# One mask product per score bank, two projection tiles behind the attention, and MLP buffers and weights placed earlier, in a transformer block on one core

## The chip, the cores and the metric

The kernel runs on one core of a Trainium2 chip. The metric is the time of one execution on the device in microseconds (us); the median over several executions counts. The engines are TensorE (PE, matrix products; its weight loads are PEld), VectorE (DVE), ScalarE (ACT), GpSimd (POOL) and SyncE (SP), whose work here is to issue transfers. Each engine takes its instructions in the order in which they were written for it, and waits at an instruction until what it needs is there; what stands behind it on the same engine waits too.

## The reference

One token sequence, S = 2048 rows of D = 576 floats, goes through an attention layer and a mixing layer with an MLP. The layer norms are modulated by six vectors that come from a condition:

```
sa, ca, ga, sb, cb, gb = split(silu(c) @ w_mod)
h = layernorm(x) * (1 + ca) + sa
q, k, v = split(h @ wqkv)                       # 32 heads of 18
p = softmax(q k^T / sqrt(18)), only 0 <= i - j < 256
x = x + ga * ((p v) @ wo)
h = layernorm(x) * (1 + cb) + sb
g = gelu(layernorm(h) @ w1)                     # 4 channel groups shifted by +1, -1, +2, -2 rows
x1 = h + shifted(g) @ w2
x = x + gb * (x1 + gelu(layernorm(x1) @ w3) @ w4)   # w3: 576 x 4608, w4: 4608 x 576
```

All is float32, and most products use operands split into a high and a low part, three products in place of one.

## The kernel before

**Stages.** By the trace they lie, in us from the start of the span: the q, k, v projections about 10 to 228; attention 228 to 738; mixing with the output projection's last tiles 740 to 958; the MLP for the first 1024 rows 958 to 1426; the MLP for the second 1024 rows 1426 to 1885. Intermediate rows go through tensors in HBM (qd, kd, vd, od, xp, hbd, xnd, xmd, rd).

**Order by a table of times.** The program has no scheduler. Every step is a small function that is entered with `at(time, function)`; at the end all entries are sorted by their time and called, and each appends its instructions to its engines' queues. The times only set an order. Inside attention the unit is one step of the head loop: `tm(h)` is the time of step h, HU = 13 units long. In the mixing stage a pair of 128-row tiles has 17.7 units, and in the MLP a block of columns has U = 24.2.

**Attention.** A step n (there are 32) is a group of 512 queries (g = n // 8) and four heads, taken as two halves j. For each half TensorE computes products mx (L448, with a mask Mq added by a product with the identity, L450), VectorE takes their maxima (L460), TensorE transposes these (mt, L468), and SyncE stores them into two rows of the query tile (L477), so that the scores proper come out with the maximum subtracted. About two steps later the scores X are computed in five PSUM banks (`xm`): each bank holds one to three key blocks (BANKS), a product each (L492), and then the mask is added: products of the identity `identr` with pieces of the mask tile Mk, which holds two 64-column halves, written over the ends of the key blocks (L517). ScalarE exponentiates each bank (L522). With all five banks there are nine mask products in a half, 576 in all. The score banks are s0 and s1 in turn. The products with the values (av, L544) follow two steps later, in banks s2 and s3, then the transposes of the outputs (ot, L554), and SyncE stores od (L566).

The query tiles have four buffers and the key tiles three. `load(n)` (L423, L425) brings both to SBUF, and POOL makes masked copies from them, QS (L431) and KS (L438), on which the mx and X products wait.

**Output projection.** `wotile(t, h)` enters all steps of one 128-row tile t: its rows from od (`orow`, L599 to L602), five transposes pa and pb (L608, L610), their evacuation into a high and a low part T (L615, L617), two halves of 14 products wo (L629), the residual (L633), two layer norms, and three stores (L655, L658, L661). Tiles 0 to 11 are entered with attention at h = 12.4 + 2t, tiles 12 to 15 with the mixing stage. All use banks s2 and s3.

**Mixing.** W1 and W2 are loaded (w1r, L740; w2r) and split into high and low parts (L752 to L757). For each pair of tiles the normalised rows come back (xmr, L780), are transposed (ptm, L787), multiplied with W1 (pg, L808), put through gelu and shifted (Gm), and multiplied with W2 (w, L857). VectorE adds the result to h (x, L861); ScalarE normalises it (xm, L873); POOL multiplies it with the gate and adds the residual (L877, L878); SyncE stores xmd (L881) and rd (L884).

**MLP.** The hidden layer is cut into 18 blocks, each of two 128-column pieces; for each block, seven products of combined rows A and combined weights W3 (u0P and so on, L1090) are added up in different ways (L1096) to the four results, a Strassen-like scheme. Gelu (L1111) and a split (L1113, L1120) give G; down products d (L1143) with W4 are added to eight accumulators acc (L1151). The raw weights of a block go through one buffer, wf (L970, L971; W4 at L975): POOL makes four differences (L982), ScalarE the high parts (L988 for W3, L1017 for W4), POOL the low parts (L994, L1023) and the gate on W4 (L1008), and VectorE a low tail (L1002). `wprep(jj, ...)` enters the preparation of block jj and the W4 part of the block before. Blocks are numbered through both halves: 0 to 17, and 18 to 35 backwards over the columns, so that block 18 reuses the W3 and W4 of block 17 and block 19 is the first that needs new W3 weights. Between the halves, `pair(1, i, ...)` loads the next 1024 token rows (rows, L1043) into the same wf buffer, POOL combines them (L1051 to L1061), and TensorE transposes them into A (pt, L1071, L1072).

## Time and profile before

| | us |
|---|---|
| median of 3 executions | 1880.74 (1880.45 to 1882.55) |
| profiled execution | 1886.33 |
| its span | 1884.5 |
| TensorE busy | 1755.3, 13752 products |
| VectorE, POOL, ScalarE busy | 1090.4, 897.1, 709.1 |
| mean granted TensorE clock | 0.963 of full |

The profile is of one execution. A busy share over the whole span mixes stages; what counts is how long TensorE stands at each place, who releases it, and at which clock it works. In the rows of a timeline the columns are: start, duration, engine, line, operation, output and inputs, shape, number of instructions in the row, and in brackets the idle time ahead of it with what ended it. The start of one product to the start of the next is what it costs in a stream; the duration of a row is longer, because products are pipelined.

### The profile page before, as it was taken

What the parts mean: (1) busy time and instruction counts of PE and PEld (TensorE: products, weight loads), DVE (VectorE), ACT (ScalarE), POOL (GpSimd) and SP (SyncE); (2) the same over time, 40 slices, a digit from 0 to 9 for tenths busy, and PEclk for the clock granted to TensorE, in tenths of its full rate; (3) what the DMA queues carried; (4) which work ended last, traced back from release to release, by engine and by line L of the source; (5) the groups of instructions that cost most, each with busy time, mean ns of one, the idle gap of its engine ahead of it and who ended that gap; (6) DMA issues with size and microseconds to landing.
All of it is one profiled execution on the core that took longest, in us unless ns stands there. A gap on an engine that the chain in (4) does not pass through costs nothing.

```text
span 1884.5 us, 34263 instructions
## 1 busy us (share of the span) xinstructions
PE 1755.3 (93%) x13752; PEld 1610.3 (85%) x13752; DVE 1090.4 (58%) x1800; ACT 709.1 (38%) x1210; POOL 897.1 (48%) x843
## 2 busy tenths in 40 slices
...
GB/s 144 316 174 182 163 145 90 117 111 131 157 131 142 146 111 103 198 204 167 122 161 58 56 58 55 57 58 57 57 69 141 59 59 59 60 59 60 58 44 51
DMA packets 156134, 206.75 MB, mean 110 GB/s; under 512 B 19012, under 2 KB 87620, under 8 KB 155400
## 3 DMA queue, kind: packets, MB, share of 16 engines
...
q14 instruction: 50, 0.41, 0.1%
...
## 4 chain that ended last, share of the span: by engine, by line
PE 45%; DVE 4%; ACT 2%; POOL 2%; issue 1%; DMA 1%; SPq 1%; DVEq 0%; POOLq 0%
PE d L1143 23%; DVE W L1002 1%; PE w L857 1%; PE pg L808 1%; PE u20P L1090 1%; PE u32P L1090 1%; PE u31P L1090 1%; PE u30P L1090 1%; PE u29P L1090 1%; PE u24P L1090 1%; PE u23P L1090 1%; PE u22P L1090 1%; PE u21P L1090 1%; PE u15P L1090 1%; PE u14P L1090 1%
## 5 line engine op out<-in xcount | busy, mean ns | idle before, releaser
L1143 PE MATMUL d<-W,G 128*128 128x288 f32 x3456 | 509.3, 298 | 13.4 <-DVE acc L1151 10.5
L1143 PEld LDWEIGHTS d<-W,G 128*128 128x128 f32 x3456 | 490.4, 190 | 35.4 <-DVE acc L1151 10.9
L1151 DVE TENSOR_TENSOR acc<-d,acc 128x576 f32<-128x576 f32 x288 | 216.7, 753 | 196.7 <-PE d L1143 194.0
L982 POOL TENSOR_TENSOR wf<-wf 128x384 f32<-128x384 f32 x140 | 144.1, 1051 | 337.0 <-DMA wf<-in_B_w_dram 328.2
L460 DVE TENSOR_REDUCE m<-mx 128x2 f32<-128x640 f32 x224 | 181.0, 817 | 171.4 <-PE mx L450 169.8
L522 ACT ACTIVATE P<-X 128x512 f32<-128x512 f32 (+4 forms) x320 | 181.9, 572 | 227.4 <-PE X L517 226.2
L448 PE MATMUL mx<-KD,QS 128*128 128x320 f32 (+4 forms) x512 | 168.0, 378 | 28.0 <-POOL QS L431 18.4
L492 PE MATMUL X<-QD,KS 128*128 128x64 f32 (+2 forms) x704 | 155.8, 312 | 1.2 <-ACT P L522 0.7
L431 POOL TENSOR_SCALAR QS<-QD,rowm 128x512 fp32r<-128x512 f32 x128 | 87.6, 697 | 145.2 <-DMA QD<-qd 51.9
L994 POOL TENSOR_TENSOR W<-wf,W 128x768 fp32r<-128x768 f32 x70 | 150.0, 2167 | 1.2 <-ACT W L988 1.2
L1120 DVE TENSOR_TENSOR G<-U,G 128x512 fp32r<-128x512 f32 x108 | 91.2, 845 | 98.8 <-ACT G L1113 98.8
L1111 ACT ACTIVATE U<-U 128x512 f32<-128x512 f32 x108 | 68.4, 633 | 184.1 <-DVE U L1096 184.1
L448 PEld LDWEIGHTS mx<-KD,QS 128*128 128x128 f32 x512 | 103.7, 202 | 34.4 <-POOL QS L431 19.5
L1111 ACT ACTIVATE C<-C 128x512 f32<-128x512 f32 x36 | 22.7, 632 | 287.3 <-DVE C L1096 287.3
L278 PE MATMUL qk<-hT,Wqk 128*128 128x512 f32 x504 | 121.3, 402 | 0.0
L278 PEld LDWEIGHTS qk<-hT,Wqk 128*128 128x128 f32 x504 | 96.1, 192 | 24.3 <-issue 0.9
L517 PE MATMUL X<-Mk,identr 128*128 128x128 f32 (+1 forms) x576 | 112.3, 269 | 0.0
L492 PEld LDWEIGHTS X<-QD,KS 128*128 128x128 f32 x704 | 108.9, 199 | 2.5 <-ACT P L522 1.8
L1008 POOL TENSOR_TENSOR wf<-wf,gb 128x1152 f32<-128x1152 f32 x35 | 104.0, 2971 | 13.3 <-DVE acc L1151 6.8
L438 POOL TENSOR_SCALAR KS<-KD,rowm 128x768 fp32r<-128x768 f32 (+1 forms) x128 | 107.6, 853 | 0.0
L1023 POOL TENSOR_TENSOR W<-wf,W 128x1152 fp32r<-128x1152 f32 x35 | 95.6, 2731 | 13.8 <-ACT W L1017 13.8
L450 PE MATMUL mx<-Mq,identr 128*128 128x128 f32 x448 | 102.0, 228 | 0.0
...
## 6 DMA issues: line engine op xcount, KB each, us to landing
...
```

Source lines behind the costliest of these rows:

```text
L278: nc.tensor.matmul(po, W[:, a, fs], H[:, c, :], start=(n == 0), stop=(n == 13))
L438: nc.gpsimd.tensor_scalar(t[:, b0:, r], src[:, b0:], M[:, 2 + r:3 + r], 0.0, op0=ALU.mult, op1=ALU.add)
L448: nc.tensor.matmul(pm[:, s, 320 - 64 * nb:320], lhs, K[:, j, 64 * (i + 5 - nb):64 * (i + 5)], start=True, stop=False)
L460: nc.vector.tensor_reduce(out=m[:, c:c + 2], in_=pm[:, :, 0:320], axis=mybir.AxisListType.X, op=ALU.max, negate=True)
L492: nc.tensor.matmul(px[:, c:c + q1 - q0], K[:, b + 4].rearrange("p r k -> p (r k)"), Q[:, j, q0:q1], start=(i == 0), stop=False)
L517: nc.tensor.matmul(o, self.identr, mv, start=False, stop=(i == len(ops) - 1))
L522: nc.scalar.activation(p[:, lo:], X["px", n, j, k][:, lo:], AF.Exp, scale=SCALE)
L982: nc.gpsimd.tensor_tensor(out=WF[:, o], in0=WF[:, a], in1=WF[:, b], op=ALU.subtract)
L994: eng.tensor_tensor(out=W[:, s0:s1, 3:5, :], in0=WF[:, 1 + s0:1 + s1, 0:2], in1=W[:, s0:s1, 0:2, :].bitcast(F32), op=ALU.subtract)
L1090: nc.tensor.matmul(po, W[:, w - 1, a, :], X[:, b, :], start=(m == 0), stop=(m == 6))
L1143: nc.tensor.matmul(po, G[:, g, ta, b, ts], W[:, w, b, cs], start=(n == 0), stop=(n == 5))
L1151: nc.vector.tensor_tensor(out=a, in0=po, in1=a, op=ALU.add)
```

## The change

1. **Masks.** Mk grows from two to five 64-column pieces (k0, k1, 0, k0, k1; one copy on VectorE more). `xm` adds the mask of a whole bank with one product: a new function `cut` returns for each bank the output columns and the piece of Mk. In four banks these are two runs of 128 columns (in the second bank of the first eight steps two of 64), in the fifth a single run. 576 products become 320. In some banks the piece k1, 0 or 0, k0 is used so that a run is 128 wide where only 64 need a mask. An unused zero tile and function are removed.
2. **End of attention.** Tiles 10 and 11 are entered at h = 33.95 and 34.5 (before 32.4 and 34.4) with banks s0 and s1, tile 12 at 35.22, tiles 13 to 15 at T1 + 6.7, 18.2 and 35.9. The mixing stage begins at tm(34.07) (before tm(34.95)), its first tile pair T1 is 19 units behind that. W1 loads come at once, the splits 5.5 units later than before, the W2 steps 5 later; the gate row gb is loaded at 15.
3. **MLP start.** The MLP begins 4 units after the last mixing pair (before 11). VectorE's tail of block 0's weights is moved behind tile 13's evacuations. The row, residual and normalised tiles of tile 15 lie in the space of the accumulators 1 to 3, in the pool m2 that is open earlier, and U1 to U3 in m2 too. The pool m3 opens, and the mixing pool closes, a little after the MLP's first step. Five accumulators are loaded at 0.2 U and three at 0.4 U.
4. **Between the halves.** `wprep` of block 19, together with the W4 part of block 17, is entered 0.3 U before block 17 (before: at 1.9 U after, with W4 alone at -0.35 U). The row loads, combinations and transposes of the second half have new times.

```diff
-        self.Mk = c.tile([P, 2, 64], F32R, name="Mk")
+        self.Mk = c.tile([P, 5, 64], F32R, name="Mk")
...
+        nc.vector.tensor_copy(self.Mk[h, 3:5], self.Mk[h, 0:2].bitcast(F32))
...
-            for i, (o, mv) in enumerate(ops):
-                nc.tensor.matmul(o, self.identr, mv, start=False, stop=(i == len(ops) - 1))
+            o, mv = cut(px, g, k, self.Mk)
+            nc.tensor.matmul(o, self.identr, mv, start=False, stop=True)
+
+        def cut(t, g, k, M):
+            pairs = lambda c, st: AP(t[:, 0:1].tensor, t[:, c:c + 1].offset, [t[:, 0:1].ap[0], (st, 2), (1, 128)])
+            mk = lambda a, w: M[:, a:a + w].rearrange("p a b -> p (a b)")
+            split = lambda m: m.rearrange("p (a b) -> p a b", a=2)
+            both = mk(0, 2).unsqueeze(1).to_broadcast([P, 2, 128])
+            sz = split(mk(1, 4))
+            if g:
+                return ((pairs(0, 256), sz), (pairs(128, 256), split(mk(0, 4))), (pairs(0, 320), both), (pairs(64, 320), both), (t[:, 192:320], mk(0, 2)))[k]
+            return ((pairs(0, 256), sz), (pairs(192, 256)[:, :, 0:64], M[:, 1:4:2]), (pairs(64, 256), sz), (pairs(128, 256), sz), (t[:, 256:320], mk(1, 1)))[k]
...
-        def otT(t):
+        def otT(t, b0):
...
-        for t in range(12):
+        for t in range(10):
             wotile(t, 12.4 + 2 * t)
-        return tm(34.0 + LX - 1.1), wotile
+        return tm, wotile
...
-            at(T0 + .1 + k, w1load, k)
-            at(T0 + 2 + 1.5 * k, w1split, k)
-            at(T0 + 12 + 2 * k, w2load, k)
-            at(T0 + 14 + 2 * k, w2split, k)
+            at(T0 + .1 + .1 * k, w1load, k)
+            at(T0 + 7.5 + 1.5 * k, w1split, k)
+            at(T0 + 17 + 2 * k, w2load, k)
+            at(T0 + 19 + 2 * k, w2split, k)
+        at(T0 + 15, lambda: nc.sync.dma_start(self.gb, self.modd[5].to_broadcast([P, D])))
...
-        return T1 + TB * (NG - 1) + 8.5, e + 11.0
+        return T1 + TB * (NG - 1) + 8.5, e + 4.0
...
+            self.late = lambda n, name: p.tile([P, D], F32, tag=f"acc{n}", name=name, bufs=1)
...
-        for i, f in enumerate((whi(0, 0, 3), wlo(0, self.nc.gpsimd, 0, 3), whi(0, 3, 7), wtail(0, self.nc.vector), wlo(0, self.nc.gpsimd, 3, 7))):
+        for i, f in enumerate((whi(0, 0, 3), wlo(0, self.nc.gpsimd, 0, 3), whi(0, 3, 7), wlo(0, self.nc.gpsimd, 3, 7))):
             at(Tc + .04 + .01 * i, f)
+        at(T0 - 7.7, wtail(0, self.nc.vector))
         add(wprep(1, 1, 0, T0 - 4.0, 11.0))
-        at(T0 - .02, begin3)
+        at(T0 + .35, begin3)
         for k in range(8):
-            at(T0 + .2 * U + .01 * k, ainit(0, (k + 4) % 8))
+            at(T0 + (.2 if k < 5 else .4) * U + .01 * k, ainit(0, (k + 4) % 8))
...
-                at(t - 0.35 * U, wload(jj + 1, None, j))
-                at(t - 0.2 * U, w4gb(jj))
-                at(t + 0.005 * U, w4hi(jj))
-                at(t + 0.01 * U, w4lo(jj))
+                if sb + 1 < SB:
+                    at(t - 0.301 * U, lambda a=jj: Ws.__setitem__(a + 1, Ws[a]))
+                    add(wprep(jj + 2, js[-2], j, t - 0.3 * U, 0.9 * U, jj))
+                else:
+                    at(t - 0.35 * U, wload(jj + 1, None, j))
...
-                    add(wprep(jj + 2, js[-2], None, t + 1.9 * U, 0.55 * U))
+                    for i, (tl, ts, td, tt) in enumerate(((.40, .52, .60, .66), (.41, .62, .92, .98), (.92, 1.06, 1.24, 1.30), (1.25, 1.38, 1.56, 1.62))):
+                        pair(1, i, t + tl * U, t + ts * U, t + tt * U, 0.25 * U, t + td * U)
...
-            T1 = te + 18.0
-            wotile(12, 35.45)
-            for i in range(3):
-                wotile(13 + i, (T1 + 17.7 * i + .5 - t1 - 6.0) / HU - 0.3)
+            T1 = te + 19.0
+            wotile(10, 33.95, 0)
+            wotile(11, 34.5, 0)
+            wotile(12, 35.22)
+            for i, d in enumerate((6.7, 18.2, 35.9)):
+                wotile(13 + i, (T1 + d - tm(0)) / HU - 0.3)
```

The change moves instructions at three places that matter below; line numbers of the changed kernel differ a little from those of the kernel before. First SyncE at the end of attention. Before (od_99 is the last group's output, od_98 in the first `or` rows the third group's; w1r are rows of W1, xmr the first mixing tiles, `or` and xr the rows of a projection tile):

```order
L566 DMA od_99<-o_9504 128x4x144
L731 DMA gb<-modd_151 128x576
L740 DMA w1r_9558<-in_B_w_dram 128x576
L740 DMA w1r_9576<-in_B_w_dram 128x576
L599 DMA or_9578<-od_99 128x576
L600 DMA or_9578<-od_99 128x64
L602 DMA xr_9581<-in_A_x_dram 128x576
L740 DMA w1r_9588<-in_B_w_dram 128x576
L740 DMA w1r_9590<-in_B_w_dram 128x576
```

and of the change (od_98 is now the last group's output, od_97 the third's):

```order
L721 DMA w1r_9188<-in_B_w_dram 128x576
L723 DMA w1r_9190<-in_B_w_dram 64x576
L724 DMA w1r_9190<-in_B_w_dram 64x576
L761 DMA xmr_9262<-xnd_131 128x576
L762 DMA xmr_9262<-xnd_131 128x64
L761 DMA xmr_9265<-xnd_132 128x576
L762 DMA xmr_9265<-xnd_132 128x64
L548 DMA od_98<-o_9234 128x4x144
L581 DMA or_9287<-od_98 128x576
```

The store of the last attention output, and behind it tile 12's rows, stood ahead of most of W1 and of the mixing tiles; they now stand behind all of W1 and the first two mixing tiles.

Second, SyncE at the start of the MLP, behind the loads of tile 15 (x_15, rr). Before:

```order
L843 DMA x_15_11955<-hbd_131 128x576
L865 DMA rr_11972<-xp_115 128x576
L881 DMA xmd_167<-xm_12000 128x576
L884 DMA rd_183<-rr_11877 128x576
L881 DMA xmd_168<-xm_12046 128x576
L970 DMA wf_12064<-in_B_w_dram 128x2x128
```

and of the change:

```order
L824 DMA x_15_11696<-hbd_130 128x576
L846 DMA rr_11713<-xp_114 128x576
L954 DMA wf_11747<-in_B_w_dram 128x2x128
L955 DMA wf_11747<-in_B_w_dram 128x1x128
...
L959 DMA wf_11747<-in_B_w_dram 128x2x576
L862 DMA xmd_166<-xm_11743 128x576
L865 DMA rd_182<-rr_11620 128x576
L862 DMA xmd_167<-xm_11801 128x576
```

The weights of block 1 (wf) stood behind the stores of tiles 13 and 14 (xmd, rd); they now stand ahead of them.

Third, SyncE between the halves of the MLP. Before, the last wf row ahead of the token rows (rows) is block 17's W4 alone, and block 19's weights come behind the output stores:

```order
L975 DMA wf_15438<-in_B_w_dram 128x2x576
L975 DMA wf_15579<-in_B_w_dram 128x2x576
L1043 DMA rows_15684<-xmd_162 128x576
L1044 DMA rows_15684<-xmd_166 128x576
L1043 DMA rows_15684<-xmd_163 128x576
L1044 DMA rows_15684<-xmd_167 128x576
```

and of the change:

```order
L959 DMA wf_15181<-in_B_w_dram 128x2x576
L954 DMA wf_15331<-in_B_w_dram 128x2x128
L955 DMA wf_15331<-in_B_w_dram 128x1x128
...
L959 DMA wf_15331<-in_B_w_dram 128x2x576
L1028 DMA rows_15482<-xmd_161 128x576
L1029 DMA rows_15482<-xmd_165 128x576
```

The eight pieces of block 19's W3 are in the same transfer group as block 17's W4, ahead of the rows that take over the buffer.

83 lines of the change are left out of this document (27 added, 56 removed).

## The prediction

> **What bounds the kernel now.** I read the busy shares first, then the table of stretches, then TensorE's waits, and last the timelines around the places that the change touches.
>
> ```profile
> PE 1755.3 (93%) x13752; PEld 1610.3 (85%) x13752; DVE 1090.4 (58%) x1800; ACT 709.1 (38%) x1210; POOL 897.1 (48%) x843
> ```
>
> No engine but TensorE is near its limit. So time is won by TensorE work that goes, by stretches in which TensorE stands, and by the halved clock that follows such stretches. The stretches say where these are (columns: stretch, then for each engine its busy time and instructions, the granted TensorE clock, the DMA share and GB/s):
>
> ```profile
> 240.00:300.00 60.00, 55.78 (x412) 52.95 (x412) 26.73 (x60) 20.61 (x44) 35.01 (x42) 0.63 0.47 132
> 300.00:400.00 100.00, 86.93 (x1155) 80.14 (x1154) 46.58 (x79) 41.08 (x84) 40.54 (x56) 0.91 0.43 114
> 400.00:500.00 100.00, 95.01 (x1246) 89.60 (x1245) 60.91 (x105) 47.13 (x89) 45.21 (x67) 1.00 0.47 136
> ...
> 740.00:780.00 40.00, 26.55 (x176) 24.51 (x175) 18.79 (x42) 16.68 (x38) 15.20 (x20) 0.83 0.63 183
> ...
> 940.00:980.00 40.00, 24.28 (x127) 21.29 (x126) 18.53 (x33) 10.12 (x12) 29.19 (x26) 0.83 0.52 175
> ...
> 1440.00:1460.00 20.00, 15.34 (x63) 12.62 (x64) 10.80 (x14) 8.56 (x12) 8.91 (x7) 0.66 0.23 70
> 1460.00:1480.00 20.00, 17.38 (x94) 15.61 (x93) 15.46 (x17) 5.46 (x8) 11.17 (x7) 0.91 0.24 70
> ```
>
> Attention runs to about 738 us. Its later part (400 to 500) is full at full clock; its first (240 to 400) has holes and a lower clock. The other holes stand at the three joints: attention to mixing (740), mixing to MLP (940), first to second half of the MLP (1440). TensorE's waits (line, who released it; total us, times, longest) name the same places:
>
> ```profile
> PE mx L448 <- POOL QS L431: 18.4, 7, 3.4
> ...
> PE wo L629 <- DVE T L617: 10.3, 10, 7.0
> ...
> PE u0P L1090 <- ACT U L1103: 9.0, 1, 9.0
> ...
> PE u19P L1090 <- POOL W L994: 3.1, 1, 3.1
> ...
> PE u19P L1090 <- DVE W L1002: 2.6, 1, 2.6
> ```
>
> **The masks.** Of 576 mask products, 256 go: four of the five score banks of a head's half had two and now have one of 256 columns (the first eight heads have one of 2x64 in the second bank). What two cost and what one of 256 columns costs is read from start to start, at full clock:
>
> ```profile
> 512.92 0.35 PE L517 MATMUL X<-Mk,identr 128*128 128x64 f32 x2
> 513.11 0.36 PE L448 MATMUL mx<-KD,QS 128*128 128x320 f32 x1
> ...
> 514.48 0.39 PE L517 MATMUL X<-Mk,identr 128*128 128x128 f32 x2
> 514.70 0.36 PE L448 MATMUL mx<-KD,QS 128*128 128x320 f32 x1
> ```
> ```profile
> 789.49 1.82 PE L808 MATMUL pg<-xT,W 128*128 128x256 f32 x14
> 791.15 0.60 PE L608 MATMUL pa<-ident,or 128*128 128x128 f32 x4
> ```
>
> Two cost 0.19 us in the first bank and 0.22 in the third; a product of 256 columns costs 1.66/14 = 0.119. That is 0.07 to 0.10 saved per pair, 0.09 on average. Heads 8 to 31 have 24 x 2 x 4 = 192 pairs: 17.3 us. TensorE is 95% busy there, but some steps wait for VectorE whatever TensorE does, so I keep 15. Heads 0 to 7 have 64 pairs, 5.8 us, but there a loop of other engines sets the pace in part. SyncE sends the maxima of one head (L477), then the transfers of the head after next, POOL waits for these, and the products for POOL:
>
> ```profile
> 323.09 1.15 SPq L477 DMA_DIRECT2D QD<-ms  x2
> ```
> ```profile
> 332.27 1.36 POOL L431 TENSOR_SCALAR QS<-QD,rowm 128x512 fp32r<-128x512 f32 x2 [8.83 <-DMA KD<-kd]
> ```
> ```profile
> 333.69 0.41 PE L448 MATMUL mx<-KD,QS 128*128 128x320 f32 x1 [3.28 <-POOL QS L431]
> ```
>
> From 323.09 to 333.69 are 10.6 us that no mask shortens; TensorE's work ahead of them it does shorten. I keep half, 3 us. **Masks: -18, between -10** (the later heads keep half, the first nothing) **and -25** (all of 23.1, and a little clock in 240 to 300, where it is 0.63).
>
> In the Trainium skill, "TensorE: Matmul & The Clock Gate", section "Back-to-back issue gap", matmuls are spaced by columns plus a constant of some 2.5 ns, about 56 ns at 128 columns and 109 at 256, when nothing but the columns counts. By that, two products of 128 columns cost as much as one of 256 and the masks give nothing; the same section warns that weight loads raise the spacing of narrow ones. The rows above, 0.22 against 0.119, bear out the warning.
>
> **The end of attention.** Projection tile 10 (28 products at L629 and five transposes) leaves its place among the last heads' scores; it and tile 11, which is behind the output transposes now, come directly behind the last value products, in the score banks; tile 12 follows. W1 loads and splits, the gate row and the second-half loads move later. Now:
>
> ```profile
> 735.59 2.90 PE L544 MATMUL av<-P,V 64*32 64x320 f32 x92
> ...
> 742.87 3.97 PE L629 MATMUL wo<-Wo,T 128*128 128x288 f32 x28 [1.13 <-DVE T L617]
> 749.45 0.63 PE L608 MATMUL pa<-ident,or 128*128 128x128 f32 x4 [2.61 <-DMA or<-od]
> ...
> 758.73 3.73 PE L629 MATMUL wo<-Wo,T 128*128 128x288 f32 x14 [6.99 <-DVE T L617]
> ...
> 767.23 0.50 PE L808 MATMUL pg<-xT,W 128*128 128x256 f32 x2 [0.68 <-ACT xT L794]
> ```
> ```profile
> 745.20 5.91 SPq L740 DMA_DIRECT2D w1r<-in_B_w_dram  x2
> ```
>
> Attention ends at 738.5 and the first product of mixing starts at 767.23: 28.7 us. In between stand tile 11 and 12 and waits of 2.6 and 7.0 us, the longer one because VectorE and ScalarE hold W1 splits ahead of the tile's own evacuation. After the change TensorE has tiles 10 and 11 at hand at once: about 13 us of products and transposes with their evacuations (an estimate: twice the 3.97 us of 28 products at 742.87, plus the transposes and a wait like the 1.13 us there for each evacuation). Meanwhile W1 is split. SyncE then issues two W1 rows that wait for splits 0 and 1, the first two mixing tiles' rows, the last attention output's store and only then tile 12's rows: by the 5.91 us at 745.20 and the issue costs around it, I put the mixing rows at 14 us, the first mixing product at 22.7 and tile 12's transposes at 22 after the last value product. That is 6.0 earlier. Tile 12's products come after it, +4.5 with their wait, less the 5.0 that tile 10 no longer takes inside attention. **-5.5, between 0** (the clock halves in both new pauses of some 4 us and takes the gain back) **and -10.**
>
> **Mixing to MLP.** TensorE's, SyncE's, VectorE's, ScalarE's and POOL's rows:
>
> ```profile
> 948.80 9.35 PE L857 MATMUL w<-W,Gm 128*128 128x288 f32 x56 [5.06 <-DVE x L861]
> ...
> 973.50 3.22 PE L1090 MATMUL u0P<-A,W 128*128 128x512 f32 x7 [8.98 <-ACT U L1103]
> ...
> 985.02 0.53 PE L1143 MATMUL d<-W,G 128*128 128x288 f32 x2 [1.53 <-ACT G L1113]
> ```
> ```profile
> 958.53 0.43 SPq L970 DMA_DIRECT2D wf<-in_B_w_dram  x1
> ```
> ```profile
> 942.64 4.62 DVE L1002 TENSOR_TENSOR W<-wf,W 32x896 fp32r<-32x896 f32 x2 [1.65 <-ACT W L988]
> ```
> ```profile
> 968.58 1.15 ACT L988 CAST W<-wf 128x1152 fp32r<-128x1152 f32 x1 [5.20 <-DMA wf<-in_B_w_dram]
> ```
> ```profile
> 963.46 1.42 POOL L877 TENSOR_TENSOR x<-x,gb 128x576 f32<-128x576 f32 x1 [0.98 <-ACT xm L873]
> ```
>
> The 5.06 us is VectorE's weight tail (4.62) standing before the evacuation that frees TensorE's bank; the change puts the tail behind it. The 8.98 us is ScalarE's copy of the first product, queued behind a cast that waits for block 1's weights; those leave SyncE only at 958.53, behind the stores of tiles 13 and 14. Now they stand ahead of these stores, and wait for the tail to free their buffer: last evacuation of tile 13 at about 944, tail to 949, issue about 949.3, 9.2 earlier. The copy then comes at 963.7 and the block goes on at 964.3 instead of 973.5. Not all of it is kept: POOL has the two gate sums of tiles 14 and 15 (four operations of 1.42 us, as at 963.46) between, and the second weight half ends by my count at 978.9. The first down product comes then instead of at 985.0. **-6, between -3 and -10.** The larger tiles kept in the MLP's pools cost nothing: they are addresses, and their eight loads are the same; three of them are issued later, after tile 15's store, and the first down products use the others.
>
> **First to second half.** Block 19's weights (the first that the second half doesn't reuse) are now prepared before block 17 ends, with block 17's down weights, not after.
>
> ```profile
> 1387.13 0.44 PE L1071 MATMUL pt<-ident,rows 128*128 128x128 f32 x2 [2.18 <-DVE U L1096]
> 1390.13 0.47 PE L1072 MATMUL pt<-ident,dup 128*128 128x128 f32 x1 [2.57 <-POOL dup L1061]
> ...
> 1440.86 2.50 PE L1090 MATMUL u19P<-A,W 128*128 128x512 f32 x5 [3.14 <-POOL W L994]
> 1445.92 0.79 PE L1090 MATMUL u19P<-A,W 128*128 128x512 f32 x1 [2.57 <-DVE W L1002]
> 1447.96 3.49 PE L1143 MATMUL d<-W,G 128*128 128x288 f32 x12 [1.24 <-ACT G L1113]
> ```
>
> The last three waits, 6.95 us, go, and with them the halved clock behind them: 0.66 over 20 us is 13.6 us at half rate, of which some 9.4 had work, so 4.6 lost. The price is at the other end: the token rows for the second half share that buffer, so they start when block 19's weights are consumed, some 3 us later by my count of POOL's work, and POOL and VectorE (one more tail of 4.6 us) work there for both. Two more down products stand ahead of the first transpose (12 matmuls of 0.14 us each, as at 742.87: 3.4 us), which covers it. If the cover fails, the waits at 1387 and 1390, 4.75 us now, grow by up to 6. The rows at 1460 to 1480 (0.91) may clear up too, up to 4 us. **-11.5, between -5 and -16.**
>
> **The sum.** 18 + 5.5 + 6 + 11.5 = 41 us off. On the profiled execution, 1886.33 us (span 1884.5), that is 1845; on the median, 5.6 us lower at 1880.74, **1840**.
>
> **Rivals.**
> A. *Attention does not get shorter.* If two mask products are not really two slots (matmul ends in the trace are modelled), or the loop of the first heads or VectorE's maxima pace the later ones as well, the 18 us are mostly not there: 1880.7 - 23 = 1858. For it: the first heads do stall 3.28 us on that loop. Against: 95% busy and full clock in 400 to 500, and start-to-start times that hold no modelled end.
> B. *The joints move but don't close.* SyncE's new queue at the end of attention and POOL's at the block boundary create waits as long as those removed; only the masks and a part of the MLP's start stay: 1880.7 - 18 - 4 = 1859. For it: tile 12's rows now stand behind two W1 loads that wait for splits.
> C. *Slower.* Place: heads 8 to 31. If they are paced by a loop, the time saved on TensorE gathers in one pause per pair of heads. A pause of 3.28 us (at 333.69) is followed by a lowered clock (300 to 400: 0.91). If the pause reaches 3 us, a half-clock window of 3 to 7 us follows and costs 1.5 to 3.5 us in each of 11 pairs: +17 to +38, with no gain from the masks: 1858 + 27 = 1885. It decides from a pause of 3 us; 16 x 0.09 = 1.4 us saved per pair plus the pauses that are there, under 1 us each, make 2.4. So: unlikely. In the Trainium skill, "TensorE: Matmul & The Clock Gate", section "What's actually happening", the clock halves after an idle window of about 3.4 us; the trace agrees with that size.
> D. *More.* The shorter first heads get their clock back sooner, and the second pause at the block boundary goes: all upper ends, 61 us, 1820.
>
> **Chances.** Forecast (1830 to 1850) 0.52; A 0.15; B 0.15; D 0.08; C 0.06; that a moved part has no effect at all because another wait ends at the same instant in several places, so that the time stays where it is, 0.04. The range, 1820 to 1864, holds the forecast, A, B and most of D. Within 0.2% of 1880.7, 3.8 us, is what a measurement can't tell from no change. C reaches from 1875 to 1896, so a sixth of it is not slower. Faster by more: 0.91; within: 0.04; slower: 0.05.
>
> **What would show it.** In the profile after: 320 mask products; 400 to 700 with the same busy share but about 1.5 us less for each pair of heads; the first mixing product within 24 us of the last value product; block 1's weight loads ahead of the stores of tiles 13 and 14 and the wait of 8.98 us below 6; no wait of u19's products, and the clock at 1.00 there. I would be wrong if the product of 256 columns takes as long as two, if the first heads' stalls grow by what the masks save, or if the transposes of the second half wait more than 4 us longer than the 4.75 us of today.

## The result, and the profile after

The changed kernel takes 1872.46 us (median of 6 executions, 1869.83 to 1875.35), the kernel before on the same chip 1882.93 us (6 executions, 1880.45 to 1888.56). The ratio is 0.9941, 95% interval 0.9923 to 0.996: faster by about 10.5 us. The forecast was 41 us, and 1872 lies above the range that it gave. The profiled execution took 1870.27 us (span 1868.5), against 1886.33 (1884.5) before. Single executions of the runs further down were disturbed (one of 2766 us, one of 3888 us); the ratios leave them out, and the trace of the first, in the first run with the old masks, is not used.

The busy shares on the page of the changed kernel:

```profile
PE 1731.3 (93%) x13496; PEld 1579.5 (85%) x13496; DVE 1094.4 (59%) x1801; ACT 707.2 (38%) x1210; POOL 902.3 (48%) x842
```

256 products fewer, as costed, and 24 us less TensorE work; but the span is only 16 us shorter, so TensorE now stands longer. The stretches of the changed kernel, cut as in the prediction (stretch, then busy time and instructions of PE, PEld, DVE, ACT and POOL, the granted clock, DMA share, GB/s):

```profile
240.00:300.00 60.00, 50.40 (x426) 46.89 (x425) 31.52 (x71) 23.12 (x50) 37.30 (x45) 0.80 0.48 138
300.00:400.00 100.00, 84.64 (x1091) 74.53 (x1090) 45.91 (x75) 40.50 (x83) 41.98 (x59) 0.88 0.42 110
400.00:500.00 100.00, 92.49 (x1197) 86.77 (x1196) 60.68 (x105) 45.70 (x87) 45.93 (x67) 0.98 0.48 139
740.00:780.00 40.00, 27.51 (x167) 26.09 (x168) 20.09 (x42) 14.97 (x33) 9.91 (x14) 0.77 0.61 193
940.00:980.00 40.00, 32.07 (x148) 27.60 (x149) 23.81 (x32) 12.35 (x16) 27.18 (x23) 0.84 0.49 155
1360.00:1400.00 40.00, 30.49 (x173) 27.48 (x172) 27.05 (x42) 15.74 (x25) 26.64 (x21) 0.87 0.22 66
1440.00:1460.00 20.00, 19.20 (x118) 17.44 (x118) 14.44 (x18) 7.67 (x11) 11.86 (x6) 1.00 0.19 53
1460.00:1480.00 20.00, 20.00 (x122) 18.16 (x121) 12.96 (x17) 6.91 (x9) 12.87 (x7) 1.00 0.10 33
```

400 to 500 was 95% busy and is 92.5%: the loss is inside the heads. The clock in 240 to 300 rose from 0.63 to 0.80, that in 300 to 400 fell from 0.91 to 0.88. The hole at 740 is as deep as it was; the one at 940 is partly filled (TensorE busy 32.1 us, before 24.3). The one at 1440 to 1480 is closed, at full clock, but a new one stands at 1360 to 1400. TensorE's waits in the changed kernel (line, releaser; us in total, times, longest) name what came in:

```profile
PE mx L444 <- POOL QS L427: 19.4, 8, 4.3
...
PE mx L444 <- DVE m L456: 10.4, 23, 0.6
...
PE w L838 <- DVE xr L615: 5.8, 1, 5.8
...
PE pt L1057 <- POOL dup L1046: 5.0, 1, 5.0
PE pg L789 <- ACT gk L801: 4.5, 2, 2.8
PE pt L1056 <- DMA rows<-xmd: 4.5, 1, 4.5
```

The wait for the maxima m was shorter and rarer in the kernel before:

```profile
PE mx L448 <- DVE m L460: 3.8, 11, 0.5
```

The others are new or have grown, at one joint or another.

**The stages side by side.** Single profiles of one kernel differ by several us in a stage: two kernels below with the same instructions up to a point are up to 5 us apart there. So the table gives every stage in every kernel of this study whose trace is used, in us between the starts of products: from the transpose mt of the maxima of step 0 to that of step 31 (attention), from there to the first product of MLP block 0 (end of attention and mixing), to block 4, block 4 to 17, 17 to 20 (between the halves), 21 to 35. The start of the MLP begins ahead of block 0, with the last W2 products of mixing, so the column "to last W1" cuts the second stage at the last product with W1 (the last pg): up to there goes to the end of attention, and what is left of the stage, together with the way to block 4, to the start of the MLP. Letters say which edits a kernel has: M the new masks, E the new end of attention, S the new start of the MLP with its buffers, B the new boundary; and, from the experiments, N layer norms moved, W the split of W2 earlier, P the old offset of W3 given back by padding, p the new offset given by padding.

| kernel | attention 0 to 31 | to last W1 | to block 0, in all | to block 4 | 4 to 17 | 17 to 20 | 21 to 35 |
|---|---|---|---|---|---|---|---|
| before | 464.1 | 233.5 | 251.7 | 103.8 | 311.1 | 105.0 | 335.1 |
| before + p | 467.4 | 228.3 | 246.3 | 103.9 | 313.8 | 101.0 | 337.4 |
| before + N | 454.8 | 229.7 | 247.8 | 102.9 | 311.1 | 104.2 | 335.1 |
| M alone | 453.2 | 228.9 | 246.9 | 103.3 | 311.1 | 103.6 | 335.1 |
| **after: M E S B** | 453.3 | 235.4 | 252.5 | 99.6 | 313.3 | 96.8 | 337.4 |
| M S B (old end) | 456.3 | 228.7 | 243.5 | 103.4 | 313.4 | 98.7 | 337.8 |
| M E B (old start) | 451.9 | 238.0 | 256.8 | 103.9 | 311.1 | 100.4 | 335.1 |
| M E S B, late transposes | 451.8 | 236.2 | 252.2 | 101.0 | 313.3 | 101.7 | 337.4 |
| the same, low parts late | 455.2 | 235.6 | 250.4 | 100.5 | 313.3 | 101.4 | 337.8 |
| M E S B + P | 455.4 | 236.2 | 251.0 | 102.7 | 311.1 | 97.9 | 335.1 |
| M E S B + W | 451.7 | 225.5 | 240.3 | 104.0 | 313.3 | 98.1 | 337.4 |
| M E S B + N | 445.5 | 235.6 | 250.4 | 102.6 | 313.3 | 98.5 | 337.4 |
| M E S B + N W P | 447.1 | 226.3 | 242.3 | 102.3 | 311.1 | 100.4 | 335.1 |
| M E S + N W P (old boundary) | 443.1 | 224.7 | 239.5 | 103.0 | 311.1 | 104.2 | 335.1 |
| E S B + N W P (old masks) | 458.5 | 225.5 | 241.4 | 100.1 | 312.2 | 99.3 | 335.1 |

### The profile page after: what moved, and what is told of

Read it like the earlier page. It is cut to its first block, busy times and chain, and to the rows that moved or that the text cites. A ratio compares the mean times of both kernels' runs of the same rounds, so it can differ in the third digit from the quotient of the medians.

```text
span 1868.5 us, 33751 instructions
## 1 busy us (share of the span) xinstructions
PE 1731.3 (93%) x13496; PEld 1579.5 (85%) x13496; DVE 1094.4 (59%) x1801; ACT 707.2 (38%) x1210; POOL 902.3 (48%) x842
## 4 chain that ended last, share of the span: by engine, by line
PE 45%; DVE 3%; POOL 3%; DMA 2%; ACT 1%; issue 1%; SPq 1%; POOLq 0%; DVEq 0%
PE d L1128 23%; PE pg L789 1%; PE w L838 1%; DVE W L986 1%; DMA wf<-in_B_w_dram 1%; PE u18P L1075 1%; PE u19P L1075 1%; PE u29P L1075 1%; PE u33P L1075 1%; PE u32P L1075 1%; PE u31P L1075 1%; PE u30P L1075 1%; PE u28P L1075 1%; PE u27P L1075 1%; PE u26P L1075 1%
## 5 line engine op out<-in xcount | busy, mean ns | idle before, releaser
L444 PE MATMUL mx<-KD,QS 128*128 128x320 f32 (+4 forms) x512 | 157.6, 358 | 38.2 <-POOL QS L427 19.4
L487 PE MATMUL X<-QD,KS 128*128 128x64 f32 (+2 forms) x704 | 151.2, 307 | 3.7 <-ACT P L504 3.3
L978 POOL TENSOR_TENSOR W<-wf,W 128x768 fp32r<-128x768 f32 x70 | 151.4, 2185 | 1.2 <-ACT W L972 1.2
L279 PE MATMUL qk<-hT,Wqk 128*128 128x512 f32 x504 | 121.0, 401 | 0.0
L1007 POOL TENSOR_TENSOR W<-wf,W 128x1152 fp32r<-128x1152 f32 x35 | 96.7, 2762 | 6.9 <-ACT W L1001 6.9
L972 ACT CAST W<-wf 128x1152 fp32r<-128x1152 f32 x70 | 90.3, 1319 | 21.6 <-DMA wf<-in_B_w_dram 10.8
```

The costliest lines, as they stand in the source:

```text
L279: nc.tensor.matmul(po, W[:, a, fs], H[:, c, :], start=(n == 0), stop=(n == 13))
L444: nc.tensor.matmul(pm[:, s, 320 - 64 * nb:320], lhs, K[:, j, 64 * (i + 5 - nb):64 * (i + 5)], start=True, stop=False)
L487: nc.tensor.matmul(px[:, c:c + q1 - q0], K[:, b + 4].rearrange("p r k -> p (r k)"), Q[:, j, q0:q1], start=(i == 0), stop=False)
L978: eng.tensor_tensor(out=W[:, s0:s1, 3:5, :], in0=WF[:, 1 + s0:1 + s1, 0:2], in1=W[:, s0:s1, 0:2, :].bitcast(F32), op=ALU.subtract)
```

## The experiments

### The masks

**The masks alone.** The kernel before with the new `Mk`, `xm` and `cut`, and nothing else of the change.

```diff
 # kernel before
-            for i, (o, mv) in enumerate(ops):
-                nc.tensor.matmul(o, self.identr, mv, start=False, stop=(i == len(ops) - 1))
+            o, mv = cut(px, g, k, self.Mk)
+            nc.tensor.matmul(o, self.identr, mv, start=False, stop=True)
```

> The kernel before with the masks alone changed (320 mask products in place of 576), nothing else. Theory A (a burst of VectorE's norm operations paces half a step in each pair of heads, so that the products saved there buy nothing): about 9 to 10 us less than before, ratio near 0.995; the pair of heads with a projection tile takes about 30.8 us in place of 31.2. Rival B (the masks alone give what was forecast, and another part of the change took it back inside attention): 15 to 18 us less, ratio near 0.991, pairs of 29.8 us. A third point: products of the MLP with 512 columns are 227 ns apart before and 231 after; if the new places of the MLP's buffers do that, they are 227 here.

Measured: 1873.29 us, ratio 0.9929 (0.9903 to 0.9956). One of the four edits gives as much as all four. Attention is 11 us shorter, not 18, and a pair of later steps takes 30.8 us on average, before 31.3: theory A. (The time alone, 8 to 18 us less by its interval, fits theory A and rival B.)

**The layer norms.** TensorE alternates in attention between a short interval from one mt to the next, 12.7 us on average in the later steps, and a long one, 18.6 us, which holds the value products of two steps. The layer norms of the projection tiles lie in the short one. In the changed kernel's first ten tiles they are moved into the long one:

```diff
-            at(tm(h + 0.90), ln1, t)
+            e = (.90, 1.25, 1.40, 1.5, 1.80, 1.95) if t > 9 else (1.67, 1.70, 1.72, 1.75, 1.90, 2.05)
+            at(tm(h + e[0]), ln1, t)
```

(and ln1n, ln2, st2, ln2n, st3 likewise with e[1] to e[5]).

> The changed kernel with the two layer norms of projection tiles 0 to 9 moved from among the maxima of a step to the stretch in which TensorE multiplies with the values and VectorE has nothing to do. Same operations, other order on VectorE. Theory A (VectorE's burst takes the masks' gain): TensorE's waits for maxima fall from 10.4 us to under 4, a pair of heads takes about 29.8 us in place of 30.8, and the whole is 6 to 10 us below the changed kernel (ratio to before about 0.990). Rival B (something else paces the pairs, such as ScalarE or the loads): the waits change their names and the time stays within 2 us of the changed kernel.

Measured: 1864.70 us, 0.9888 (0.9844 to 0.9931); attention 445.5 us against 453.3. TensorE's waits for the maxima all but go (10.4 us in the changed kernel), and those for QS, 17.5 us between 240 and 745 in the changed kernel, grow. In the kernel with the layer norms moved, over the same stretch:

```profile
PE mx L444 <- POOL QS L427: 31.1, 15, 3.8
```

That seemed to show that the masks' missing part lay hidden behind VectorE. It needed the opposite test.

**The layer norms without the masks.** The same move in the kernel before.

> The kernel before with one thing from the repairs: the ten early projection tiles' layer norms moved to the stretch of probabilities times values. Theory (in the old heads VectorE and TensorE are nearly level, so that either alone saves little more than half, and the masks' 18 us need both): the last maxima come 2 to 6 us earlier than in the kernel before, the time is 1877 to 1883 us. Rival (VectorE alone paces the heads with a projection tile, with the old masks as with the new, and the masks' other half was never there): the last maxima 8 to 11 us earlier, the time 1871 to 1876 us.

Measured: 1874.35 us, 0.9945 (0.9924 to 0.9967); the last maxima 9.9 us earlier. The theory, that either alone saves little, is wrong: moving the layer norms gives 7 us over the steps 12 to 31 whatever the masks are (means over the table's kernels: 295.0 to 288.0 us with the old masks, 289.5 to 282.4 with the new). One short and one long interval, stretch by stretch, of the kernel before:

```profile
506.00:518.71 12.71, 11.76 (x90) 11.25 (x90) 9.90 (x17) 6.23 (x11) 5.07 (x10) 1.00 0.59 166
518.71:537.20 18.49, 17.79 (x312) 16.97 (x312) 8.97 (x16) 8.18 (x16) 9.22 (x12) 1.00 0.37 107
```

of the changed kernel:

```profile
501.88:514.49 12.61, 11.12 (x82) 10.47 (x82) 9.90 (x17) 6.14 (x11) 5.07 (x10) 1.00 0.60 169
514.49:532.69 18.20, 17.33 (x304) 16.24 (x304) 8.97 (x16) 8.18 (x16) 9.24 (x12) 1.00 0.37 107
```

of the kernel before with the layer norms moved:

```profile
499.53:511.27 11.74, 11.27 (x90) 11.12 (x91) 6.82 (x9) 6.24 (x11) 2.82 (x4) 1.00 0.61 170
```

and of the changed kernel with the layer norms moved:

```profile
494.14:506.07 11.93, 10.55 (x82) 10.35 (x82) 6.82 (x9) 6.14 (x11) 3.22 (x5) 1.00 0.64 169
```

The number behind the stretch is its length, the interval; the next is TensorE's busy time. In the short interval the masks take eight products and 0.64 us from TensorE (11.76 to 11.12) and 0.10 from the interval (12.71 to 12.61): VectorE, busy 9.90 us there, sets its length. VectorE's rows of the changed kernel show it: after one wait it has next to no pause to the end of the interval, with the residual and two layer norms between the maxima.

```profile
504.89 0.82 DVE L456 TENSOR_REDUCE m<-mx 128x2 f32<-128x640 f32 x1 [2.33 <-PE mx L446]
...
508.62 0.82 DVE L456 TENSOR_REDUCE m<-mx 128x2 f32<-128x640 f32 x1 [0.15 <-PE mx L446]
509.36 1.02 DVE L624 SCALAR_TENSOR_TENSOR h<-xr,b3mv,cb 128x576 f32<-128x576 f32 x1
...
512.93 2.44 DVE L456 TENSOR_REDUCE m<-mx 128x2 f32<-128x640 f32 x3
```

With the layer norms gone VectorE is busy 6.82 us, and the interval falls to 11.74 with the old masks and 11.93 with the new (11.98 and 11.83 on average): still hardly a gain from the masks. In the changed kernel with the layer norms moved it is the copy QS on GpSimd that TensorE then waits for, in this interval as in the totals above:

```profile
494.14 0.28 PE L464 MATMUL mt<-ident,m 128*16 128x128 f32 x1 [0.41 <-DVE xr L615]
...
505.50 0.42 PE L444 MATMUL mx<-KD,QS 128*128 128x320 f32 x1 [1.38 <-POOL QS L427]
506.07 0.27 PE L464 MATMUL mt<-ident,m 128*16 128x128 f32 x1
```

In the long interval the masks take 0.46 us from TensorE and 0.29 from this interval; on average over the nine long ones of steps 12 to 31 the interval falls from 18.63 to 18.16, by all of it. So TensorE saves three quarters of what was forecast (0.55 us a step on average; eight pairs at 0.09 are 0.72), and the time gets it in half of the steps: the short intervals fall by 0.09 us on average.

### The end of attention

**The old end.** The changed kernel with the projection tiles 10 to 15, their banks, T1 and the times of W1, W2 and gb as before (the main lines).

```diff
-        for t in range(10):
+        for t in range(12):
...
-            at(T0 + 7.5 + 1.5 * k, w1split, k)
-            at(T0 + 17 + 2 * k, w2load, k)
+            at(T0 + 2 + 1.5 * k, w1split, k)
+            at(T0 + 12 + 2 * k, w2load, k)
...
-            te = tm(34.07)
+            te = tm(34.95)
...
-            wotile(10, 33.95, 0)
-            wotile(11, 34.5, 0)
-            wotile(12, 35.22)
...
+            wotile(12, 35.45)
```

> The changed kernel with the end of attention as before: tiles 10 to 12 at their old places, old banks, old times of W1, W2 and the gate row; the masks, the MLP's start and the boundary stay changed. Theory A (the new order of that stage loses as much as it wins, since W2's rows wait behind the next tiles for the three staging buffers): the time is equal to the changed kernel or up to 4 us below it. Rival B (the moved tiles do win 5 us, and the loss lies elsewhere): 4 to 6 us above it.

Measured: 1866.86 us, 0.9876 (0.9838 to 0.9914): faster than with the new end, by more than the 4 us of the theory; 243.5 us against 252.5 from the last maxima to the MLP. The changed kernel's TensorE rows in that place:

```profile
740.67 0.66 PE L768 MATMUL ptm<-ident,xmr 128*128 128x128 f32 x4 [3.81 <-DMA xmr<-xnd]
...
746.87 5.60 PE L789 MATMUL pg<-xT,W 128*128 128x256 f32 x28
...
757.17 2.51 PE L789 MATMUL pg<-xT,W 128*128 128x256 f32 x14 [2.84 <-ACT gk L801]
...
777.39 6.07 PE L838 MATMUL w<-W,Gm 128*128 128x288 f32 x28 [5.82 <-DVE xr L615]
```

The first mixing product starts at 746.87, 23.1 us after the last value product (723.8), where the forecast had 22.7. Then it goes wrong: the product with W2 starts only at 777.39, 4.5 us earlier than in the kernel before, though pg is 20.4 earlier. Attention's earlier end is in both: counted from the last value product, pg comes 5.9 us earlier (23.1 against 28.9) and the W2 product 10.0 us later (53.6 against 43.6). ScalarE, SyncE and VectorE of the changed kernel tell why:

```profile
753.59 0.68 ACT L752 CAST W<-w2r 128x576 fp32r<-128x576 f32 x1 [5.80 <-DMA w2r<-in_B_w_dram]
754.28 1.28 ACT L801 ACT_TABLE_LOAD   x1
...
772.57 0.67 ACT L755 CAST W<-w2r 128x576 fp32r<-128x576 f32 x1 [5.41 <-DMA w2r<-in_B_w_dram]
```
```profile
760.11 0.32 SPq L761 DMA_DIRECT2D xmr<-xnd  x1
...
767.31 3.58 SPq L747 DMA_DIRECT2D w2r<-in_B_w_dram  x8
```
```profile
773.34 0.76 DVE L756 SCALAR_TENSOR_TENSOR w2r<-W,w2r 128x576 f32<-128x576 f32 x1 [4.75 <-DMA hbd<-h]
...
776.79 0.45 DVE L615 TENSOR_TENSOR xr<-wo,xr 128x288 f32<-128x288 f32 x1
```

The W2 rows share three staging buffers with the rows xmr of the second pair of mixing tiles, which now stand ahead of W2's tail; the buffer comes free when these are transposed (766.2), so the eight tail loads leave at 767.31. ScalarE sits 5.8 and 5.4 us in front of its casts; behind the first stands gk, behind the last VectorE's split of W2's tail (773.34, idle 4.75 us before), and behind that the evacuation L615 that the first W2 product waits for.

**W2 earlier.** The changed kernel with the W2 loads ahead of those rows.

```diff
-            at(T0 + 17 + 2 * k, w2load, k)
-            at(T0 + 19 + 2 * k, w2split, k)
+            at(T0 + (9.6, 9.65, 9.85, 14, 16)[k], w2load, k)
+            at(T0 + (16.5, 16.7, 17, 18, 24.5)[k], w2split, k)
```

> The changed kernel with W2's loads and splits ahead of the loads of the second pair of mixing tiles and of tile 13's rows; the rest of the end of attention stays as changed. Theory A (W2's last rows share three staging buffers with the mixing tiles, so they wait for a transpose that TensorE does late, and the first W2 product waits for them): the wait of 5.8 us ahead of the first W2 product goes and that product comes 5 to 9 us earlier than in the changed kernel. Rival B (the stage is paced by tile 12 and the evacuations, not by W2): another wait takes its place and the first W2 product comes within 2 us of where it does.

Measured: 1861.09 us, 0.9879 (0.9846 to 0.9912). The tail loads leave at 745.73, the wait at the first w product is 0.38 us in place of 5.82, that product comes 7.3 us earlier counted from the last maxima, and the stage takes 240.3 us. SyncE's and TensorE's rows of this kernel:

```profile
745.73 4.40 SPq L747 DMA_DIRECT2D w2r<-in_B_w_dram  x8
```
```profile
766.56 4.05 PE L838 MATMUL w<-W,Gm 128*128 128x288 f32 x28 [0.38 <-DVE xr L615]
```

So with W2 ahead the new end is better than the old one (225.5 us to the last W1 product, old end 229.8 on average); the W2 times that came with the change cost more than that. Whether W2 ahead would help the old end as well was not run.

### Between the halves of the MLP

TensorE's, SyncE's and GpSimd's rows of the changed kernel:

```profile
1382.52 0.41 PE L1056 MATMUL pt<-ident,rows 128*128 128x128 f32 x2 [4.50 <-DMA rows<-xmd]
1387.94 0.47 PE L1057 MATMUL pt<-ident,dup 128*128 128x128 f32 x1 [5.01 <-POOL dup L1046]
```
```profile
1379.21 0.34 SPq L1028 DMA_DIRECT2D rows<-xmd  x1
```
```profile
1370.21 5.92 POOL L978 TENSOR_TENSOR W<-wf,W 128x768 fp32r<-128x768 f32 x2
1376.09 3.10 POOL L1007 TENSOR_TENSOR W<-wf,W 128x1152 fp32r<-128x1152 f32 x1
```

The three waits at block 19 are gone. But the token rows leave when GpSimd has used the weights in their buffer, block 19's W3 (L978) and last block 17's W4 (L1007, to 1376.09 + 3.10 = 1379.19), and TensorE, 10 us earlier than before, now stands 9.5 us at the transposes where it stood 4.75, and its clock halves behind that: 0.87 over 1360 to 1400. From the first product of block 18 to that of block 20 the change takes 52.0 us down to 36.7, but from block 17 to 18 it goes from 53.0 to 60.1.

**Transposes later.** The changed kernel with the second half's transposes behind block 17's down products, which are there to be done (of each line the part that differs).

```diff
-((.40, .52, .60, .66), (.41, .62, .92, .98), (.92, 1.06, 1.24, 1.30), (1.25, 1.38, 1.56, 1.62)), 0.25 * U
+((.40, .52, .60, 1.01), (.41, .62, 1.18, 1.21), (1.19, 1.28, 1.38, 1.41), (1.39, 1.48, 1.58, 1.61)), 0.16 * U
```

> The changed kernel with the transposes for the second half of the MLP put behind six down products in place of two, and closer together; nothing else. Theory A (the rows come late because block 19's weights hold their buffer, and TensorE stands for them with down products still at hand): the waits of 4.5 and 5.0 us and the half clock behind them go, block 18 starts 6 to 10 us earlier. Rival B (the chain of the row pairs itself, load, sums, copy, transposes, sets the start of block 18): the wait moves to a later pair and block 18 starts within 3 us of where it does.

Measured: 1878.64 us, 0.9951 (0.9929 to 0.9973), and 101.7 us from block 17 to 20 against 96.8. The products put ahead have a wait of their own, 7.7 us for an accumulator (VectorE still has block 17's sums and block 19's tail in front of it), and the fourth pair's combined rows come late. TensorE's rows of this kernel:

```profile
1383.98 7.93 PE L1128 MATMUL d<-W,G 128*128 128x288 f32 x48 [7.73 <-DVE acc L1136]
...
1416.06 0.47 PE L1057 MATMUL pt<-ident,dup 128*128 128x128 f32 x1 [4.58 <-POOL dup L1046]
```

**The low parts later too.** The same with VectorE's low parts of block 17's G moved back, so that the accumulators come first.

```diff
-(q(n, 0.08), glo(jj, ta, b))
+(q(n, 0.08) if jj != NJ - 1 else t0 + dt * (1.28 + .191 * (n - 3)), glo(jj, ta, b))
```

> The kernel with the late transposes (down products first), and in addition VectorE's low parts of block 17's gelu output moved behind the first accumulations of block 16; no other order changes. Theory A (TensorE waits there for VectorE, which still has the weight tail and block 17's chain of sums and low parts in front of the accumulations that free TensorE's banks): the wait of 7.7 us ahead of the third down product goes, and block 18 starts 5 to 8 us earlier than with the late transposes alone, about 3 us earlier than in the changed kernel. Rival B (the chain of the row pairs sets it): the wait moves to the transposes and block 18 starts within 2 us of the kernel with the late transposes.

Measured: 1874.95 us, 0.9944 (0.9924 to 0.9964), 101.4 us. The 7.7 us wait is down to 0.4; that for the fourth pair's combined rows stays (4.55 us at 1411.96), their loads behind output stores on SyncE. Each order that was tried moves the wait. GpSimd itself stands 8.35 us for these loads, so what sets the length of the stage is not shown.

### The start of the MLP, and where its buffers lie

From block 4 on the changed kernel loses 0.167 us a block against the kernel before (313.30 against 311.13 us for 13 blocks), with TensorE busy throughout and no wait. The starts of the up products, 512 columns each, are 228.8 ns apart on average in the kernel before (in a group of seven about 231 three times, then 227 three times), 232.1 in the changed one (229 and 226, then 235 and 231 in turn). No instruction of these blocks differs; the two tiles W3 do lie elsewhere: 101344 and 119264 bytes into each partition before, 85792 and 103712 after. Modulo 512 that is 480 and 288.

**W3 moved by 320 bytes.** The changed kernel with an unused tile behind the two.

```diff
             W3.extend(p.tile([P, 7, 5, P], F32R, name=f"W3_{n}") for n in range(2))
+            p.tile([P, 80], F32, name="pad")
```

> The changed kernel with 320 unused bytes per partition behind the two W3 buffers, so that these lie at the same place within 512 bytes as before the change; no instruction differs. Theory A (the spacing of the MLP's 512-column products, 231 ns against 227 before, depends on where their weights lie): back to 227 ns, a block of the MLP takes 23.93 us in place of 24.09, 5 us in all. Rival B (it depends on what the other engines read and write beside them, whose buffers moved too): 231 ns as in the changed kernel, and the time is the same.

Measured: spacing back at 228.8, in the old pattern, 13 blocks in 311.13 us, no drift; total 1871.82 us, 0.993 (0.9904 to 0.9956), so in the total the few us are not resolved.

**The opposite.** The kernel before with 192 bytes there, so that W3 lies at 288 modulo 512.

> The kernel before with 192 bytes behind the two W3 tiles and nothing else: they lie 192 bytes lower, at the offset within 512 bytes (288) that they have in the changed kernel, and no instruction, wait or load differs. Theory (the place of W3 alone sets the spacing of the up products): 231 ns instead of 227 from the first block on, blocks of 24.09 us instead of 23.93, a drift of 0.16 us a block that ends near +5.6 us at the last product. Rival (the spacing comes from something else in the changed kernel, say the other buffers' places or the transfers' times, and the 320 bytes that cured it did so by accident): 227 ns, and the time is that of the kernel before within 0.2%.

Measured: the same pattern and mean (232.1) as in the changed kernel, 313.75 us for 13 blocks (changed kernel 313.30) and 337.40 for 14 more (337.40). The time is 1889.67 us, 1.0016 (0.9998 to 1.0034): the drift is there, but in this profile the stage between the halves is 4 us shorter than in the kernel before, and the interval holds no change as well as the 5.6 us that were expected. The up products of one block, busy us and mean duration of one in ns, in the kernel before:

```profile
L1090 PE MATMUL u8P<-A,W 128*128 128x512 f32 x49 | 12.4, 392 | 0.0
```

and in the kernel before with 192 bytes of padding:

```profile
L1091 PE MATMUL u8P<-A,W 128*128 128x512 f32 x49 | 12.5, 394 | 0.0
```

**The start undone.** The changed kernel with the MLP's pools, W3's place and the load of block 1's weights as before.

```diff
-        return T1 + TB * (NG - 1) + 8.5, e + 4.0
+        return T1 + TB * (NG - 1) + 8.5, e + 11.0
...
-        at(T0 + .35, begin3)
+        at(T0 - .02, begin3)
```

(and the accumulators, U1 and dst in the later pool, the tail of block 0 as before).

> The changed kernel with the start of the MLP undone: its pools opened and closed when they were before, the accumulators and the buffers U1 and dst back in the later pool, the weights of the second block loaded at the old time. Theory (the new place of the buffers costs what the earlier start gives): the W3 tiles are back at their old addresses, so the up products are 227 ns apart again instead of 231 and the blocks 4 to 17 keep a constant distance to the kernel before (no drift of 0.16 us a block, about 5.6 us in 36 blocks); the distance from the first product of the MLP to the fourth block goes back from 99.6 to about 103 us; the time lies within 3 us of the changed kernel. Rival (the forecast's term: the earlier start is worth 6 us, and nothing else hangs on it): the time is 6 us above the changed kernel's, and the up products keep their 231 ns.

Measured: 1875.81 us, 0.9932 (0.9908 to 0.9957), beside 0.993 of the kernel with the new start and W3 at the same offset. The difference of the two is uncertain by 7 us, so the times decide nothing; the stages do. From the last W1 product to block 4 the old start takes 122.7 us here (121.0 to 122.7 in the five kernels that have it), the new one 117.5 in that kernel (115.3 to 118.8 in ten). The spacing is 228.8 again, W3 being back in its old place. So the theory fits: the start gives 4.5 us on average, and the place of W3 takes as much (below). The waits did move as forecast. TensorE's rows of the changed kernel:

```profile
957.87 1.90 PE L1075 MATMUL u0P<-A,W 128*128 128x512 f32 x7 [0.84 <-ACT U L1088]
963.85 6.25 PE L1075 MATMUL u0P<-A,W 128*128 128x512 f32 x14 [4.08 <-DVE U L1081]
974.60 1.72 PE L1128 MATMUL d<-W,G 128*128 128x288 f32 x11 [2.74 <-POOL W L1007]
```

The 8.98 us for ScalarE's copy is 0.84, and the next wait, for VectorE's sum, has grown from 1.67 to 4.08. Counted from the last W1 product, the first down product comes 8.2 us earlier on average (45.1 to 36.9) and block 4 comes 4.5 earlier: blocks 0 to 3 give nearly half of it back. What holds them is not shown; GpSimd takes 22 to 24 us from one block's weights to the next there, but stands 7 to 8 us of that for their loads.

### The three together, and the price of two parts in that kernel

**Layer norms, W2 and W3's place.** The edits N, W and P in the changed kernel at once.

> The changed kernel with the three repairs together that were run one at a time before: the ten early projection tiles' layer norms moved to the stretch of probabilities times values, the split of W2 loaded ahead of the modulation tiles, and 320 bytes behind the two W3 tiles. Theory (three separate causes: VectorE between the maxima, the chain that splits W2, the place of W3): the gains add up. In the profiles they were 8.0 us (-24.06 against -16.08 at the last product), 8.7 us, and for the place of W3 a steady block spacing that is worth 0.16 us over each of some 35 blocks, about 5 us; together about 20 us below the changed kernel, so a time of 1850 us (1847 to 1856), the last maxima about 22 us earlier than in the kernel before, the first product with w about 25 us earlier, and no drift between the fourth and the seventeenth block. Rival (the start of the MLP takes back what comes early, because GpSimd prepares the first blocks' weights at its own pace): the gains up to the first MLP product are kept, but the distance from there to the fourth block grows from 99.6 to over 106 us and the time stays above 1858 us.

Measured: 1851.12 us (5 executions, 1843.47 to 1854.03), the kernel before beside it 1887.85; 0.9802 (0.9777 to 0.9828). In the time the three add up, as the theory said, and there is no drift; the last maxima come 16.4 us earlier than in the kernel before and the first W2 product 21.5, where it expected 22 and 25. The start of the MLP takes nothing back that stands out (102.3 us from block 0 to 4). This version beats both kernels: it is 1.4% faster than the changed one by the two ratios. The hole at the end of attention in this kernel:

```profile
740.00:780.00 40.00, 38.88 (x300) 37.95 (x300) 27.15 (x63) 21.87 (x49) 14.60 (x25) 0.98 0.73 237
```

**Its masks undone**, twice (with `Mk`, `xm` as before):

```diff
+            for i, (o, mv) in enumerate(ops):
+                nc.tensor.matmul(o, self.identr, mv, start=False, stop=(i == len(ops) - 1))
-            o, mv = cut(px, g, k, self.Mk)
-            nc.tensor.matmul(o, self.identr, mv, start=False, stop=True)
```

> The kernel with the three repairs, and the masks of before in it (eight narrow products a half, or fourteen instructions where they were, for one product a bank). It prices the masks where TensorE paces the attention. Theory (the forecast's term was of the right size, and VectorE between the maxima hid half of it): the last maxima come about 16 to 20 us later than with the three repairs (-16.45 against the kernel before), that is near the kernel before, and the time is 1866 to 1872 us. Rival (the masks are worth only the 10 us that they gave alone, and moving the layer norms saves the rest by itself): the last maxima 8 to 11 us later, a time of 1859 to 1863 us.

> The kernel with the three repairs and the old masks once more, for a profile that is not disturbed and a closer time. Theory (with VectorE out of the way the masks are worth what the forecast said): the last maxima 16 to 20 us later than with the three repairs, the time 16 to 20 us above it. Rival (the masks give 10 us with or without the layer norms between the maxima): the last maxima 8 to 11 us later, the time 8 to 11 us above.

Measured: 0.9871 (0.9836 to 0.9907), and in the second run 1864.37 us, 0.9888 (0.9861 to 0.9915). Against 0.9802 that is 13 and 16 us, each uncertain by 7 to 8; by the trace of the second run attention is 458.5 us against 447.1, 11.4 us. The trace speaks for the rival; the times alone do not decide.

**Its boundary undone.**

```diff
-                    at(t - 0.301 * U, lambda a=jj: Ws.__setitem__(a + 1, Ws[a]))
-                    add(wprep(jj + 2, js[-2], j, t - 0.3 * U, 0.9 * U, jj))
+                at(t - 0.35 * U, wload(jj + 1, None, j))
...
+                    add(wprep(jj + 2, js[-2], None, t + 1.9 * U, 0.55 * U))
```

(and the second half's loads, sums and transposes at the old times).

> The kernel with the three repairs, and the boundary between the MLP's halves as before (the weights of the second half's first new block loaded behind the boundary, the activations of the second half loaded and transposed at the old times). Theory (the new boundary gives back part of what it saves): 8 us slower than with the three repairs (the change gained 8.2 from the seventeenth to the twentieth block in the profile), 1857 to 1861 us; the stalls at the nineteenth and twentieth block are back (about 7 us with their half clock), the stalls at the second half's first transposes are 4 to 5 us instead of about 9.5. Rival (the forecast's full term is there when TensorE comes early): 11 us or more.

Measured: 1852.84 us (three executions), 0.9834 (0.9791 to 0.9878). Against 0.9802 that is 6 us, uncertain by 10, so the times don't decide; the stage takes 104.2 us against 100.4, 3.8 us where the theory had 8. The waits at block 19 are back as in the kernel before:

```profile
1407.40 2.10 PE L1077 MATMUL u19P<-A,W 128*128 128x512 f32 x5 [3.15 <-POOL W L980]
1412.48 0.80 PE L1077 MATMUL u19P<-A,W 128*128 128x512 f32 x1 [2.97 <-DVE W L988]
```

The boundary's full term is not there even when TensorE comes early: less than half of it is.

## Why the prediction was wrong

Sizes below are means over the kernels of the table that lack an edit and those that have it (without N for the masks, without W for the end, the two reordered boundaries left out). Their sum, 10.7 us, is near the 10.5 measured.

| term | forecast | shown |
|---|---|---|
| masks, heads 8 to 31 (maxima of step 9 to 31) | -15 | -7.6 (344.2 to 336.6) |
| masks, heads 0 to 7 (maxima of step 0 to 9) | -3 | -4.6 (121.6 to 117.0) |
| end of attention (to the last W1 product) | -5.5 | +6.3 (229.8 to 236.1) |
| start of the MLP (from there to block 4) | -6 | -4.5 (121.8 to 117.3) |
| boundary between the halves | -11.5 | -4.8 (103.6 to 98.8) |
| place of W3 | not seen | +4.5 (2.2 + 2.3, blocks 4 to 17 and 21 to 35) |
| sum | -41 | -10.7 |

(The scores of a head are computed about two steps behind its maxima, so the first two rows are cut at step 9; heads 30 and 31 come behind the last maxima and are in neither.)

**Masks: the step that failed is "some steps wait for VectorE whatever TensorE does, so I keep 15".** The price per pair, 0.09 us, was a little high: TensorE's busy time fell by 0.64 us in a short interval and 0.46 in a long one, 0.08 and 0.06 for each of eight pairs. What failed is how much of it the time gets. In each interval with a projection tile's layer norms VectorE sets the length, so half of the steps gave next to nothing, and a pair of steps 0.6 us in place of the 1.5 named as a sign; 95% busy and full clock in 400 to 500 did not show that, because the products that wait for a bank there wait a few tenths of a us each, 3.8 us in all, and the busy share still looked full. Rival A named the mechanism, VectorE's maxima that "pace the later ones as well", with 1858 us and a chance of 0.15; it was the right one for half of the later steps. The layer norms moved show what VectorE cost there, 7 us, with the old masks as with the new. Behind VectorE stands GpSimd's QS. Heads 0 to 7 gave 4.6 us, more than the 3 forecast, though kernels of the same masks differ there by 3 to 4.5 us; how much of it is the loop through SyncE and GpSimd, and how much the clock, was not separated. No pause of the size that rival C needs gathers in the later heads (longest wait in 400 to 500: 0.6 us, clock 0.98), so rival C did not come about.

**End of attention: the step that failed is the sum that ends at the first mixing product.** That product came as forecast (23.1 us after the last value product; 22.7 forecast). The forecast then took its 6 us as won, and added tile 12 (its terms, -6.0, +4.5 and -5.0, make -6.5, not the -5.5 that it kept). It did not follow the W2 steps, which the edit moves too ("the second-half loads move later" stands there with no price), past the rows that share their staging buffer. Undone, the end is better; with W2 ahead of the rows it takes 225.5 us on average (four kernels), 4.3 less than the old end's 229.8: most of the 5.5 us of the forecast was to be had. Rival B, "SyncE's new queue at the end of attention", was right here, with tile 12's rows named in place of W2's.

**Start of the MLP: the term held.** The wait for ScalarE's copy fell as the forecast said, below 6 (0.84), and block 1's loads stand ahead of the stores. The forecast kept 6 of 9.2 us; 4.5 are there at block 4, inside its bounds of 3 and 10, and 8.2 at the first down product. In the total it does not show, because the place of W3 takes 4.5 us.

**Placement: "they are addresses" is the step that failed.** The forecast costed the larger tiles in the MLP's pools at nothing. They moved W3 by 15552 bytes, and its new offset lengthens an up product from 228.8 to 232.1 ns on average over 27 blocks: 49 products a block make 0.16 us, the drift.

**Boundary: the cover failed, with a price inside the forecast's own bound.** The waits at block 19 and their half clock went as costed, and the last stretch's clock is full. Two down products (3.4 us) were to cover the later rows. They did not: the rows came 2 us earlier, but TensorE 10 us earlier, and the two waits grew from 4.75 to 9.5 us, with half clock behind them. "More than 4 us longer" was the sign named for being wrong, and it is there. The forecast reckoned GpSimd's delay from the old time of TensorE's arrival, although its own other terms moved that by 29.5 us.

**In one sentence**: each of the four terms was a sum over what goes away, made as if the other engines came earlier as well; three of them met, within the interval or some us later, an engine or a buffer whose pace had not changed (VectorE, W2's staging buffers, the weights' buffer that the token rows share), a fifth term was not seen, and rivals A and B, 0.15 each, both happened in part at once. (A slip in the chances: of rival C's 1875 to 1896 nearly half, not a sixth, is not slower; it moves them by under 0.02.)
